# One PSUM pool with banks in fixed turns for the prologue and the first loop of a long-convolution and maxout kernel, with the first loop's tables loaded later

## The chip, the cores and the metric

The kernel runs on one core of a Trainium2 chip. A core has a matrix engine (PE, TensorE), three engines for element-wise work (DVE or VectorE, ACT or ScalarE, POOL or GpSimd), a queue engine that issues transfers (SP or SyncE), a working memory (SBUF) and a small memory that matrix products are written to (PSUM). PSUM is used here as eight banks of 128 partitions x 512 fp32. Every engine works through its own list of instructions in order; semaphores hold an instruction back until those it depends on are done. The metric is the device time of one execution in microseconds (us), the median of several runs.

## The reference

All arrays are fp32. A filter is made of a small network and a decaying window, convolved with u = x * v along the sequence (length S = 12544, four batches, 128 channels), gated with x, and fed to a maxout layer:

```
h_mlp  = np.maximum(pos_emb @ w1, 0.0) @ w2            # (S, 128), pos_emb is (S, 64)
h_filt = h_mlp * np.exp(-0.01 * pos)[:, None]
u = x * v                                              # (4, S, 128)
y = irfft(rfft(u, 2*S) * rfft(h_filt, 2*S)[None], 2*S)[:, :S]
a = (x * y).reshape(4*S, 128)
out = np.maximum(np.maximum(a @ m1, a @ m2), a @ m3) @ m_out   # m1..m3: (128, 768)
```

The weights m1 to m_out come in as float64 and are turned into fp32 on DVE.

## The kernel before

The Fourier transforms are matrix products with tables, in two stages (sizes 90 and 128). The order of the work is that of the program: each engine gets its instructions in the order in which the code writes them down, and a layer above the hardware adds the semaphore waits. It keeps them by tile: a tile from a pool is a piece of SBUF or PSUM with a name; when a pool of `bufs` tiles hands out a piece again, the new writer waits for the readers of the old one, and when a pool is closed and another opened in its place, the new one's tiles wait for all that used the old piece.

*Prologue* (before.py up to L989). PE makes the filter's network (`mlp_in`, L334; two PSUM tiles `pms` of two banks each, memset at L291) while the first units of u are loaded, multiplied on DVE (`u_mul`, L374), transposed on PE (`turn2`, L900; L379) and taken through the first stage (`early`, L918). This uses the pool `fps0`, closed at L957. A second pool `fps` (L958) has four tiles of two banks. In it run 16 products of the filter (`quad`, L909, with `first_halves`, L159: PE at L165, copy on ACT at L174 into `specH`), then the units u = 4 to 31 in pairs (two `quad`, then a `turn2` for a later pair; copies into `spec`). Each pair frees SBUF for a pair of loads (`u_load`, L362) that SP issues. Between them DVE converts the weights (`some`, L886), whose raw data POOL's queue loads. Ahead of the units, SP also issues the six first tables of the first loop (L972 and L973: `wf` and `wi`, 256 KB each, `load_dir`, L895). L994 closes the pool.

*First loop* (L1096, s = 0 to 47, NK = 45). It does the second stage, the product with the filter, and the first stage back, for one batch, two frequencies per step. It has three PSUM pools (L998 to L1000): `cps0` with three banks, `sps` with one tile of two banks (tag h) and one of one bank (tag pl), and `gps` with two banks. In step s, in this order on PE:

- `s_second(s)` (L1028, "ss"): the filter's second stage into a bank of `gps`, copied by ACT (G, L1042)
- `g_second(s)` (L555, "even product" in the text): u's second stage, PE at L156, into a bank of `cps0`; ACT copies half of it (eo, L192)
- `s_filter(s-1)` (L1045): the filter's last product, PE at L1055 into the tile h, copied by ACT (ht, L1071; for the last step L1064)
- `g_third(s-3)` (L592, "third product"): the stage back, PE at L156, into a bank of `cps0`; ACT copies it (zs, L603) and SP stores it to `zd`

ACT also swaps halves (xs, L570 and L571, for s-1). DVE does the multiplication with the filter for s-2 (L576, L580, L581), the unfolding (ab, L588) and then the butterfly of s (`g_butterfly`, L562; L186 and L187, which read the even product's bank). POOL negates a table (L1025) and stores ht. In steps 36, 37, 41 and 42 a unit of the next batch is also transposed (`u_turn`, L379) into the bank pl, and in some steps multiplied (L374).

*End of the loop* (L1133 to L1145). The last third products (of 42, 43 and 44) alternate with two late units (`unit`, L1091: two calls of `u_products`, L417, each 16 products at L427, a copy on ACT at L439, two sums on DVE at L443) and with `fold` (L1015), which multiplies m1 with m_out: transposes into a bank (L1017), a copy (w1t, L1019), a product into pl, and a last copy into `lin` (L1144). The banks for units and turns come from `banks_of` (L1001), a fixed list of six.

*Second loop and last part* (from L1148, some 310 us to the end) are not touched. Its tiles are loaded from `zd` once the last third product is stored.

Of the kernel before, what the change touches and what calls it, by code (L numbers as in the profile page):

```python
# [10 lines left out]
FP32 = mybir.dt.float32  # L11
# [4 lines left out]
PSUM = bass.MemoryType.PSUM  # L16
P = 128
# [14 lines left out]
def e(t):  # L32
    return np.exp(2j * np.pi * (t - np.floor(t)))


def stacked(c):

    top = np.concatenate([c.real, c.imag], -1)
    bottom = np.concatenate([-c.imag, c.real], -1)
    return np.concatenate([top, bottom], -2)  # L40


def tables(NB):
    S = P * N1
    k1 = np.arange(N1).reshape(2, N1 // 2).T.ravel()
    n = np.arange(NB)
    a = e(np.outer(n, k1 + 0.25) / N1)
    f1 = np.concatenate([a.real, a.imag], 1)
    up = e(np.outer(n + 0.5, k1 + 0.25) / N1)
    f1q = np.stack([np.concatenate([up.real, up.imag], 1), f1], 1)  # L50
    f1h = np.zeros((64 + HH, 2, 2 * N1))
    f1h[:HH, 0], f1h[64:, 0] = f1[:HH], f1[HH:NH]
    f1h[:HH, 1], f1h[64:, 1] = f1[HH:NH], f1[:HH]
    f4 = np.stack([a.T.real, a.T.imag], 1) / S
    f4p = f4[::2].transpose(1, 0, 2).reshape(N1, NB // 2, 2).transpose(0, 2, 1)
    f4 = np.stack([up.T.real, up.T.imag], 1) / S
    f4s = f4[::2].transpose(1, 0, 2).reshape(N1, NB // 2, 2).transpose(0, 2, 1)
    f4q = np.stack([f4p, f4s * np.array([1, -1])[:, None]], 1)
    j, t = np.arange(64), np.arange(64)
    tw = (k1[:, None, None] + 0.25) / S  # L60
    half = []
    for r in range(2):
        s2 = (127 - 2 * t - r)[None, :, None]
        half.append(stacked(e(tw * s2 + j[None, None, :] * s2 / 128)))
    fwd = np.stack(half, 2)
    half = []
    for q in range(2):
        s2 = (2 * t + q)[None, None, :]
        half.append(stacked(e(-tw * s2 - j[None, :, None] * s2 / 128)))
    inv = np.stack(half, 2)  # L70
    both = np.stack([fwd, inv], 2)
    both = both.reshape(N1 // 2, 2, P, 2, 256).transpose(0, 2, 3, 1, 4)
    both = both.reshape(N1 // 2, P, 2, 512)
    j, t = np.arange(32), np.arange(32)
    quarter = [[], []]
    for v in range(2):
        for w in range(2):
            s2 = (63 - 2 * t - v)[None, :, None]
            quarter[0].append(stacked(e(tw * s2 + (2 * j + w)[None, None, :] * s2 / 128)))
            s2 = (2 * t + w)[None, None, :]  # L80
            quarter[1].append(stacked(e(-tw * s2 - (2 * j + v)[None, :, None] * s2 / 128)))
    quarter = np.stack([np.stack(q, 1) for q in quarter], 1)
    quarter = quarter.reshape(N1 // 2, 2, 2, 2, 2, 64, 64).transpose(0, 3, 5, 2, 1, 4, 6)
    quarter = quarter.reshape(N1 // 2, P, 2, 256)
    steps = np.zeros((N1 // 2 + LATE, P, 2, 256))
    steps[:N1 // 2, :, 0], steps[LATE:, :, 1] = quarter[:, :, 0], quarter[:, :, 1]
    f32 = np.float32
    return tuple(np.ascontiguousarray(t, f32) for t in (f1q, f1h, f4q, both, steps))


@with_exitstack
def kernel(
# [21 lines left out]
    NK = N1 // 2  # L114
# [139 lines left out]
    pro = ExitStack()  # L254
# [5 lines left out]
    fin = ExitStack()  # L260
    inp0 = fin.enter_context(tc.tile_pool(name="inp0", bufs=3))
    sml = fin.enter_context(tc.tile_pool(name="sml", bufs=1))
    mps = ExitStack()
    fps = mps.enter_context(tc.tile_pool(name="fps0", bufs=2, space=PSUM))

# [18 lines left out]
    warm = sml.tile([P, 256], FP32, name="warm")  # L286
    nc.vector.memset(warm[:], 0.0)
    nc.vector.memset(win, 0.0)
    pms = [fps.tile([P, 1024], FP32, name=f"pm{i}", bufs=1) for i in range(2)]
    for pm in pms:  # L290
        nc.vector.memset(pm[32:64], 0.0)  # L291
    for h in range(2):
# [37 lines left out]
    def w2_order():  # L330
        nc.scalar.copy(w2x[:].rearrange("f (c g) -> f c g", c=GC),
                       w2_in[:].rearrange("f (g c) -> f c g", c=GC))
# [24 lines left out]
    def pools(b, u):  # L357
        if b == 0:
            return inp0 if u % 2 else inp
        return inp if u < EARLY or u % 4 < 3 else inq  # L360

    def u_load(b, u):  # L362
        c, g0 = divmod(u, NG // 4)
        ts = []
        for src in (xr, vr):
            t = pools(b, u).tile([P, 4, NB], FP32, tag=f"u{len(ts)}", name="ut")
            nc.sync.dma_start(
                t[:], src[4 * g0:4 * g0 + 4, :, c, b, :].rearrange("g p n -> p g n"))
            ts.append(t)
        us[u] = ts  # L370

    def u_mul(u):
        a, v = us[u]
        nc.vector.tensor_tensor(out=a[:], in0=a[:], in1=v[:], op=ALU.mult)  # L374
# [511 lines left out]
    def some(n):  # L886
        for _ in range(n):
            if not todo and jobs:
                todo.extend(convert(raws.pop(0), *jobs.pop(0)))
                if len(jobs) > 1:  # L890
                    raws.append(load_raw(*jobs[1], nc.gpsimd))
            if todo:
                todo.pop(0)()

    def load_dir(g, a):  # L895
        w = lwp.tile([P, 2, 2, P], FP32, tag=f"w{a}", name="wt")
        nc.sync.dma_start(w[:].rearrange("p k r m -> p (k r m)"), wt_d[g, :, a, :])
        return w
# [55 lines left out]
    for u in (0, 2):  # L954
        uts.pop(u)
    w2_order()
    mps.close()  # L957
    fps = fin.enter_context(tc.tile_pool(name="fps", bufs=4, space=PSUM))  # L958
    for f in range(0, FO, 4):
        quad([hs[:, f + i] for i in range(4)], (f1h[:, 0], f1h[:, 1]), specH[:, :, :, f:f + 4])  # L960
        u, k = divmod(f // 4, 4)
# [7 lines left out]
        some(2 if u < 2 and k < 2 else 3)  # L969
    for u in range(4):  # L970
        nc.gpsimd.tensor_copy(spec[:, 0:NS, :, 4 * u:4 * u + 4], aside[u])
    wf = {g: load_dir(g, 0) for g in range(3)}  # L972
    wi = {g: load_dir(g, 1) for g in range(3)}  # L973
    for u in range(4, NU, 2):
        t = uts.pop(u)
        for v in range(2):
            if u + 4 < NU:
                u_mul(u + 4 + v)
            at = 4 * (u + v)
            quad([t[:, 4 * v + i] for i in range(4)], (f1, f1), spec[:, :, :, at:at + 4])  # L980
            some(1)
        if u + 4 < NU:
            turn2(u + 4)
        for v in (u + 10, u + 11):
            if v < NU:
                u_load(0, v)
        some(2)
    while todo or jobs:
        some(1)  # L989
# [5 lines left out]


    cvp = pro.enter_context(tc.tile_pool(name="cvp0", bufs=3))
    cps = pro.enter_context(tc.tile_pool(name="cps0", bufs=3, space=PSUM))  # L998
    sps = pro.enter_context(tc.tile_pool(name="sps", bufs=1, space=PSUM))
    gps = pro.enter_context(tc.tile_pool(name="gps", bufs=2, space=PSUM))  # L1000
    def banks_of():  # L1001
        for pool, tag, n in ((gps, "g", 1), (gps, "g", 1), (sps, "h", 2), (gps, "g", 1),
                             (cps, "cv", 1), (gps, "g", 1)):
            yield pool.tile([P, 512 * n], FP32, tag=tag, name="ps1")[:, 0:512]

    free = banks_of()

    def bank():
# [36 lines left out]
    def s_filter(g):  # L1045


        G = Gs.pop(g)
        ps = sps.tile([P, 1024], FP32, tag="h", name="sps")
        for ri in range(2):  # L1050
            for k in range(2):
                for q in range(2):
                    for h in range(2):
                        at = 512 * q + (2 * ri + k) * D
                        nc.tensor.matmul(  # L1055
                            ps[64 * h:64 * h + 64, at:at + D],
                            G[64 * q:64 * q + 64, k, ri, :], w2x[64 * q:64 * q + 64],
                            start=(ri == 0 and k == 0), stop=True, skip_group_check=True)
        v = ps[:].rearrange("p (q m d) -> p m q d", q=2, d=D)
        if g == NK - 1:  # L1060
            hts[g] = []
            for c in range(2):
                ht = lwp.tile([P, 2, 2, D], FP32, tag="w0", name="ht")
                nc.scalar.copy(ht[:], v[:, 2 * c:2 * c + 2])  # L1064
                hts[g].append(ht)
            return
        if g % 2 and g < NK - 11:
            ht = utp.tile([P, 2, 2, 2, D], FP32, tag="uT", name="ht")
        else:
            ht = cvp.tile([P, 2, 2, 2, D], FP32, tag="ht", name="ht", bufs=2)  # L1070
        nc.scalar.copy(ht[:].rearrange("p r k q d -> p (r k) q d"), v)  # L1071
        hts[g] = ht[:, 0], ht[:, 1]
# [23 lines left out]
    for s in range(NK + 3):  # L1096
# [9 lines left out]
        if 1 <= s <= NK:  # L1106
            g_swap(s - 1)
            s_filter(s - 1)
# [22 lines left out]
        if s == NK:  # L1131
            unit(0)
            pl = sps.tile([P, 512], FP32, tag="pl", name="pl")  # L1133
# [27 lines left out]
    cps = conv.enter_context(tc.tile_pool(name="cps", bufs=1, space=PSUM))  # L1161
# [15 lines left out]
    for n, (b, i) in enumerate(tiles[:LAST]):  # L1177
# [13 lines left out]
        for f in range(NF):  # L1191
# [9 lines left out]
            h = up((b, i), f)  # L1201
# [25 lines left out]
    cps = ctx.enter_context(tc.tile_pool(name="cps2", bufs=1, space=PSUM))  # L1227
# [19 lines left out]
    for i in range(0, NT, 2):  # L1247
        h = {}
        X, Y = banks if i % 4 == 0 else banks[::-1]
        for j, (name, f) in enumerate(ORDER):  # L1250
            n = int(name[1]) - 1
# [64 lines left out]
```

## Time and profile before

| what | us |
|---|---|
| median of 3 runs | 2277.69 |
| lowest and highest run | 2275.16, 2278.18 |
| the profiled execution, its own time | 2277.68 |
| its span, first to last instruction | 2275.9 |
| PE busy in it | 2255.8 |
| prologue, first instruction to last unit's product | 0 to 114.3 |
| first loop with its end | 114.3 to about 303 |

How to read it: a page of the profile gives busy times by engine, and the chain of work that ended last. The chain by time lists start, length, and what ran ("PE ps L165 x96": 96 matmuls of line 165 into the tile ps); "issue" is time in which the engine waited for nothing that the profile shows. The timeline gives start, length, engine, line, operation and tiles, and in brackets the idle time before it and who ended that. A line of busy times by stretch gives the stretch, its length, the busy time of PE, of PE's weight loads, of DVE, ACT and POOL with their counts of instructions, then the granted clock of PE (1.00 is full), the busy share of the DMA engines and GB/s. "PEld" is PE's weight load; "SPq" a transfer's issue on SP.

### The profile page before, as it was taken

To read this page: it belongs to the slowest core of one execution; us is meant where nothing else is said; L and a number is where in the kernel's file an instruction comes from. 1 tells how busy PE (TensorE), PEld (TensorE's weight loads), DVE (VectorE), ACT (ScalarE), POOL (GpSimd) and SP (SyncE) were. 2 spreads that over 40 slices of the span, in tenths; PEclk is the share of its full clock that TensorE was granted. 3 is DMA by queue.
4 is the path that set the end of the run, shared out by engine and by line. 5 is a ranking of instruction groups with operands and counts; after the bars stand their busy time and mean duration, and the time that the engine had idled before them with its cause. 6 is when DMAs were issued, how large, how long until landed. Compare 5 with 4: busy or idle time off the path is not lost.

```text
span 2275.9 us, 68490 instructions
## 1 busy us (share of the span) xinstructions
PE 2255.8 (99%) x27855; PEld 1380.2 (61%) x27855; DVE 1560.6 (69%) x2856; ACT 1175.8 (52%) x2130; POOL 879.4 (39%) x1089
## 2 busy tenths in 40 slices
PE   9999999999999999999999999999999999999998
PEld 7889866655555556655555556655555546666665
DVE  5589967677777757667878757658878754544443
ACT  3688844466666534456666534456666522222222
POOL 1045434323333334323333333423333326666666
PEclk9999999999999999999999999999999999999999
DMA  8778999799989689889999789979999732222221
GB/s 197 174 227 279 301 198 181 138 220 239 249 219 238 172 174 185 160 194 251 236 240 233 197 167 180 168 183 247 238 236 238 199 81 56 56 71 65 58 56 22
DMA packets 473365, 411.03 MB, mean 181 GB/s; under 512 B 327993, under 2 KB 374522, under 8 KB 473050
## 3 DMA queue, kind: packets, MB, share of 16 engines
q1 hardware_dynamic: 446034, 329.50, 65.2%
q0 software_dynamic: 26224, 75.44, 11.1%
q8 instruction: 219, 3.59, 0.7%
q10 hardware_dynamic: 792, 1.72, 0.3%
q14 instruction: 96, 0.79, 0.1%
HBM read 262.84 MB, written 84.67 MB: 153 GB/s over the span
## 4 chain that ended last, share of the span: by engine, by line
PE 96%; DVE 1%; issue 0%; ACT 0%; DMA 0%; SPq 0%; POOL 0%; POOLq 0%; DVEq 0%; ACTq 0%
PE hps L156 44%; PE ops L156 19%; PE ops L827 6%; PE cps L427 5%; PE cps L156 4%; PE ps L156 4%; PE cps L494 3%; PE cps L504 3%; PE ps L165 3%; PE sps L1055 2%; PE gps L1037 2%; PE last L156 1%; PE pst L379 1%; DVE spec L443 0%; DMA xT<-in_x_dram 0%
## 5 line engine op out<-in xcount | busy, mean ns | idle before, releaser
L156 PE MATMUL hps<-gt,w_sb 128*64 128x392 f32 x6144 | 1149.6, 494 | 0.0
L764 ACT ACTIVATE hid<-hps 128x392 f32<-128x392 f32 x768 | 384.0, 500 | 698.2 <-PE hps L156 679.8
L156 PEld LDWEIGHTS hps<-gt,w_sb 128*64 128x64 f32 x6144 | 432.6, 137 | 419.4 <-issue 391.5
L767 DVE TENSOR_TENSOR hid<-hid,hps 128x392 f32<-128x392 f32 x768 | 428.4, 558 | 331.2 <-PE hps L156 319.1
L156 PE MATMUL ops<-hid,wo_sb 128*64 128x392 f32 x2304 | 480.6, 492 | 0.0
L546 POOL TENSOR_TENSOR cb<-cb,xs 128x512 f32<-128x512 f32 x135 | 174.1, 1290 | 463.5 <-DVE xs L543 339.7
L156 PEld LDWEIGHTS ops<-hid,wo_sb 128*64 128x64 f32 x2304 | 173.1, 137 | 206.1 <-issue 206.1
L519 DVE TENSOR_TENSOR cb<-cps,eo 128x512 f32<-128x512 f32 (+1 forms) x288 | 175.3, 650 | 73.4 <-ACT eo L516 73.4
L443 DVE TENSOR_TENSOR spec<-cps,high 128x360 f32<-128x360 f32 x188 | 140.1, 786 | 117.7 <-ACT high L439 117.5
L782 POOL DMA_DIRECT2D out_dram<-ot x96 | 75.3, 785 | 345.3 <-ACT ot L780 311.0
L534 ACT ACTIVATE xs<-cb 32x512 f32<-32x512 f32 x270 | 169.6, 628 | 20.6 <-DVE cb L519 11.6
L535 ACT COPY xs<-cb 32x512 f32<-32x512 f32 x270 | 166.3, 616 | 3.2
L439 ACT COPY high<-cps 128x360 f32<-128x360 f32 (+1 forms) x94 | 74.9, 796 | 176.0 <-PE cps L427 140.6
L550 DVE TENSOR_TENSOR xs<-cb 128x256 f32<-128x256 f32 x270 | 140.9, 567 | 9.5 <-POOL cb L546 9.2
L427 PEld LDWEIGHTS cps<-f1q,uT 98*64 98x64 f32 x2992 | 130.2, 137 | 27.8 <-issue 25.0
L427 PE MATMUL cps<-f1q,uT 98*64 98x90 f32 x2992 | 134.4, 241 | 1.7 <-DVE spec L443 0.5
L395 POOL COPY planes<-ut 128x784 uint16<-128x784 uint16 x90 | 76.3, 848 | 144.7 <-DVE ut L374 144.7
L527 POOL DMA_DIRECT2D zd<-cb x135 | 92.7, 687 | 62.0 <-DVE cb L519 57.3
L156 PEld LDWEIGHTS cps<-f4p,even 90*64 90x64 f32 x1552 | 90.1, 138 | 34.8 <-issue 34.0
L851 POOL DMA_DIRECT2D out_dram<-o x128 | 77.7, 612 | 51.8 <-DVE o L844 49.6
L156 PE MATMUL cps<-f4p,zt 90*64 90x49 f32 x1552 | 96.4, 222 | 0.0
L156 PE MATMUL cps<-f4p,even 90*64 90x49 f32 x1552 | 95.1, 220 | 0.0
(146 smaller groups left out, 3156.4 us busy)
## 6 DMA issues: line engine op xcount, KB each, us to landing
ht<-hd SPq DMA_DIRECT2D x264, 256.0 KB, 7.0
wt<-wq_const SPq DMA_DIRECT2D x144, 256.0 KB, 6.3
zd<-cb POOLq DMA_DIRECT2D x135, 256.0 KB, 6.3
zt<-zd SPq DMA_DIRECT2D x384, 90.0 KB, 3.0
sq<-spec SPq DMA_DIRECT2D x264, 128.0 KB, 7.0
ut<-in_xr_dram SPq DMA_DIRECT2D x128, 196.0 KB, 4.0
ut<-in_vr_dram SPq DMA_DIRECT2D x128, 196.0 KB, 4.2
xT<-in_x_dram SPq DMA_DIRECT2D x256, 98.0 KB, 3.4
```

The source lines that it names most:

```text
L156: nc.tensor.matmul(out[64 * h:64 * h + 64], lhsT[:, 64 * h:64 * h + 64], rhs, start=start, stop=stop, skip_group_check=True)
L427: nc.tensor.matmul(ps[64 * c:64 * c + 64, 256 * i + h * N1:256 * i + (h + 1) * N1], t[:, 2 * ((at + i) % 8) + h].rearrange("n r t -> n (r ...
L443: nc.vector.tensor_tensor(out=spec[:, :, a, at:at + n], in0=v[:, 1], in1=highs[0], op=op)
L519: nc.vector.tensor_tensor(out=cb[:, a, lo:hi], in0=ps[:, lo:hi], in1=eo[:, lo:hi], op=op)
L527: nc.gpsimd.dma_start(zd[b][2 * z:2 * z + 2].rearrange("k c t a f -> (k c t) a f"), zss.pop(z))
L534: nc.scalar.mul(xs[at:at + 32], xt[at + 32:at + 64], -1.0)
L535: nc.scalar.copy(xs[at + 32:at + 64], xt[at:at + 32])
L546: nc.gpsimd.tensor_tensor(out=xts[g], in0=xts[g], in1=xs[:], op=ALU.add)
L550: nc.vector.tensor_tensor(out=ab[:, q], in0=y[:, 0], in1=y[:, 1], op=(ALU.subtract, ALU.add)[q])
L764: nc.scalar.activation(h[:], pa[:, 0:N], Relu)
L767: nc.vector.tensor_tensor(out=h[:], in0=h[:], in1=pb[:, 0:N], op=ALU.max)
L827: nc.tensor.matmul(ps[64 * c:64 * c + 64, 0:H2], w, rhs[:, H2 * c:H2 * c + H2], start=start, stop=True, skip_group_check=True)
```

## The change

All eight banks are taken once, as four tiles of two banks each, `acc[0]` to `acc[3]`, from one pool that lives until the end of the first loop. `half[0]` to `half[7]` are their halves, one bank each. A small class `Banks` has the method of a pool, `tile`, but hands out given pieces in fixed turns. The tiles of the first loop are halves: even and third products take turns through half[2], half[3], half[4]; ss through half[0] and half[1]; the filter's product is acc[3], and in the last step acc[0]; pl is half[5]; `banks_of` gives half[6], half[7], half[0], half[1], one of half[2..4], half[6]. The six tables are issued on SP after the loads of units 30 and 31 (in the iterations u = 22, 24 and 26) in place of ahead of all units.

```diff
+class Banks:
+    def __init__(self, **tags):
+        self.tags = {tag: itertools.cycle(aps) for tag, aps in tags.items()}
+
+    def tile(self, shape, dtype, tag, name):
+        return next(self.tags[tag])
...
-    mps = ExitStack()
-    fps = mps.enter_context(tc.tile_pool(name="fps0", bufs=2, space=PSUM))
+    acc = pro.enter_context(tc.tile_pool(name="acc", bufs=1, space=PSUM))
+    acc = [acc.tile([P, 1024], FP32, name=f"acc{i}")[:] for i in range(4)]
+    half = [a[:, 512 * i:512 * i + 512] for a in acc for i in range(2)]
+    fps = Banks(cv=acc[:2])
...
-    pms = [fps.tile([P, 1024], FP32, name=f"pm{i}", bufs=1) for i in range(2)]
+    pms = acc[2:]
...
-    mps.close()
-    fps = fin.enter_context(tc.tile_pool(name="fps", bufs=4, space=PSUM))
+    fps = Banks(cv=acc[2:] + acc[:2])
...
-    wf = {g: load_dir(g, 0) for g in range(3)}
-    wi = {g: load_dir(g, 1) for g in range(3)}
+    wf, wi = {}, {}
...
+        if u in (22, 24, 26):
+            wf[(u - 22) // 2] = load_dir((u - 22) // 2, 0)
+            wi[(u - 22) // 2] = load_dir((u - 22) // 2, 1)
...
-    cps = pro.enter_context(tc.tile_pool(name="cps0", bufs=3, space=PSUM))
-    sps = pro.enter_context(tc.tile_pool(name="sps", bufs=1, space=PSUM))
-    gps = pro.enter_context(tc.tile_pool(name="gps", bufs=2, space=PSUM))
+    cps, gps, sps = Banks(cv=half[2:5]), Banks(g=half[0:2]), Banks(h=[acc[3]], pl=[half[5]])
+
     def banks_of():
-        for pool, tag, n in ((gps, "g", 1), (gps, "g", 1), (sps, "h", 2), (gps, "g", 1),
-                             (cps, "cv", 1), (gps, "g", 1)):
-            yield pool.tile([P, 512 * n], FP32, tag=tag, name="ps1")[:, 0:512]
+        yield from half[6:8] + half[0:2]
+        yield cps.tile([P, 512], FP32, tag="cv", name="ps1")
+        yield half[6]
...
-        ps = sps.tile([P, 1024], FP32, tag="h", name="sps")
+        ps = sps.tile([P, 1024], FP32, tag="h", name="sps") if g < NK - 1 else acc[0]
```

## The prediction

> **What bounds the kernel now.** I read the whole page first (busy times, chain), then the chain by time, then busy times by stretches, then the timeline of one step of the first loop and of its end.
>
> ```profile
> PE 2255.8 (99%) x27855; PEld 1380.2 (61%) x27855; DVE 1560.6 (69%) x2856; ACT 1175.8 (52%) x2130; POOL 879.4 (39%) x1089
> ...
> PE 96%; DVE 1%; issue 0%; ACT 0%; DMA 0%; SPq 0%; POOL 0%; POOLq 0%; DVEq 0%; ACTq 0%
> ```
>
> PE is the bound from end to end: any time in which it waits in the first 310 us moves the end by as much, and no more than PE's waits there can be won. The chain by time and the stretches show where they are:
>
> ```profile
> 50.23 9.45 PE ps L165 x239
> 59.68 2.15 issue
> ...
> 114.28 0.77 ACT spec L174
> 115.04 0.04 issue
> 115.09 0.43 PE gps L1037 x2
> 115.52 0.51 issue
> ```
>
> ```profile
> 59.60:61.90 2.30, 0.15 (x4) 0.07 (x3) 0.00 (x0) 0.27 (x1) 0.00 (x0) 1.00 1.10 322
> 61.90:65.80 3.90, 3.90 (x60) 3.90 (x61) 3.77 (x11) 1.24 (x2) 0.67 (x2) 0.56 0.28 66
> 65.80:69.00 3.20, 3.20 (x67) 2.91 (x63) 0.42 (x1) 1.81 (x3) 1.75 (x4) 1.00 0.18 24
> ```
>
> PE stops at 59.68 for 2.15 us in the middle of a product, waiting for no semaphore, with the DMA engines full (1.10), and then runs 3.9 us at a granted clock of 0.56. At 114.28 it waits for the last copy of the pool that is closed. A third stop (0.92 us, before 39.16) is at the first pool's close.
>
> The first loop has no such stop. One step, g = 193.02 being the start of its even product:
>
> ```profile
> 193.02 1.04 PE L156 MATMUL ps<-spec,wt 128*64 128x128 f32 x16
> ...
> 194.16 0.37 ACT L192 COPY eo<-ps 128x256 f32<-128x256 f32 x1 [0.35 <-PE ps L156]
> ...
> 195.84 1.01 ACT L1071 COPY ht<-sps 128x1024 f32<-128x1024 f32 x1
> ...
> 196.16 0.42 DVE L186 TENSOR_TENSOR xt<-eo,ps 128x256 f32<-128x256 f32 x1
> ...
> 196.75 0.59 ACT L603 COPY zs<-ps 128x512 f32<-128x512 f32 x1
> 196.82 1.04 PE L156 MATMUL ps<-spec,wt 128*64 128x128 f32 x16
> 196.89 0.69 DVE L576 TENSOR_TENSOR xt<-xt,ht 128x512 f32<-128x512 f32 x1
> ```
>
> PE's step is 3.81 us. ACT ends its step (zs) only at 197.34 = g+4.32, after the next product began; DVE starts at 193.08, ends its butterfly at 196.91 = g+3.89, and starts the next chain at 196.89. All three engines are full, and run staggered because every product has a bank that nobody else holds.
>
> [...] ACT reads one bank at 196.75 while PE writes another. So a wait between the two halves of a two-bank tile is not asked for by the chip. [...] here 2.15 us of idleness were followed by 0.56. [...] the page's instruction queue q8 has 219 packets in 3.59 MB (16.4 KB each), and the DMA view has none of them in 52 to 58 us and one in 58 to 60[...].
>
> **The change, part by part.**
>
> 1. *First pool's close.* The last copy no longer gates the first filter product: it goes to acc[2], free and with its inputs ready when DVE has done the last MLP tile (36.97), and PE is there at 38.24. The 0.92 us go: -0.9. PE is late in nothing else there (inputs of the next transposes are multiplied by 38.5).
>
> 2. *Tables moved.* Six loads of 256 KB (1.57 MB) leave 51.9 to 55.2[...]. At about 250 GB/s that is 6.3 us of DMA[...]. The stop (2.15) goes, and with it the slow clock: 113 matmuls took 6.23 us from 61.83, at the 0.0411 of 2.63/64 they are 4.64, so 1.6. Together -3.7. The SP queue now issues them behind the last input loads, at about 99; DMA is idle from 104 to 118 (share 0.00 to 0.03), and the first is needed at 114, so they land in time. Price if their cover fails: [...]0 to +3.7. I take 0.
>
> 3. *Start of the loop.* The first filter product needs only acc[0], copied long before, so it starts at 114.25 instead of 115.09, and the 0.51 of queued waits are hidden behind it. The built order of the second even product shows a new wait for the first one's butterfly; it starts at about 117.6 instead of 118.76: -1.1.
>
> 4. *Banks as halves of four tiles.* Here is what the diff doesn't tell. In the built program, waits are made by tile, and half[2], half[3] are one tile (acc[1]), half[4] and half[5] another. Even product s and third product s-3 take turns through half[2..4], with a period of three steps. The built waits of steps 5, 6, 7 (with their producers):
>
> ```
> step 5  even  -> acc1  waits ACT zs of third(1)      new
> step 6  even  -> acc1  waits DVE butterfly of 5      new
> step 6  DVE butterfly  waits ACT zs of third(3)      new
> step 7  even  -> acc2  no wait
> ```
>
> None of these is in the kernel before. Worked out with the offsets of the step above:
> - Steps 5, 8, ... : zs ends at g+4.32, ACT to PE takes 0.05 (267.03+1.01 to 268.09), so the next product starts at g+4.37, not 3.81: +0.56. There are 14 (5 to 44); at 38 a transpose covers it: 13 x 0.56 = 7.3.
> - Steps 6, 9, ... : the butterfly starts at g+4.37 instead of 3.14. DVE, which has no slack (its chain from L576 to butterfly is 3.08, and 0.73 more to the next L576), carries this lag through step 7 to step 8: L576 at g+5.10, then +3.81 to the next L576, then 3.08 + 0.75 to the end of that butterfly. With the steps 3.81 and 4.37 in between this is 4.56 after product 8, +0.14 from DVE to PE (305.72 to 305.86), 4.70 instead of 3.81: +0.89. There are 13 (6 to 42); 39 and 42 are covered by transposes: 11 x 0.89 = 9.8.
> - Transposes (L379) go to half[5], one tile with half[4]. Steps 36 and 42: the next even product waits for the transpose's copy (ends at g+4.81): g+4.86 instead of 4.53, +0.33 each. In step 37 the transpose waits for the butterfly (g+4.02, +0.14) instead of starting at g+2.93: +1.23; in step 41 for zs (g+4.37): +1.44. Sum 3.3. A multiplication (L374, 0.56) ahead of one such butterfly: +0.5.
> Sum of the loop: +20.9.
>
> 5. *End of the loop.* The last filter product saves its 0.79 of waiting, but DVE and ACT set that stretch, so 0 is won. The first late unit's two halves are now half[6] and half[7], one tile, and the second half waits until DVE has added up the first:
>
> ```profile
> 289.63 1.41 PE L427 MATMUL ps<-f1q,uT 98*64 98x90 f32 x32
> ...
> 291.27 1.09 PE L156 MATMUL ps<-ab,wt 128*64 128x128 f32 x16 [0.23 <-DVE xt L576]
> ...
> 293.73 1.09 DVE L443 TENSOR_TENSOR spec<-ps,high 128x180 f32<-128x180 f32 x4
> 293.76 1.09 PE L156 MATMUL ps<-ab,wt 128*64 128x128 f32 x16
> ```
>
> Behind that PE wait are queued the last two third products, at 291.27 and 293.76. The first half's adds end at about 294.3, +0.7 for DVE's lag; so the first of them goes from 291.27 to about 295.8, the second (behind a fold that waits for zs) from 293.76 to about 298.3: +4.5. Their stores, the reload and the second loop follow. The other unit has the same wait (+1.2) and the folds wait for each other's copies (+0.8). PE idles some 5.5 us, more than the 2.15 that cost it its clock: +0.7 as a middle of 0 to 1.7. Together +7.
>
> After 310 us nothing differs; what is late stays late.
>
> **Sum.** -0.9 -3.7 -1.1 +20.9 +7 = +22.2. The profiled execution took 2277.68 us (span 2275.9), the median of the three runs is 2277.69: 2299.9, I say 2300. Unknown costs: the lag on DVE 0 to 9.8, the clock 0 to 1.7, the end 4 to 8[...].
>
> **Rivals.**
> - *The half-tile waits are there but covered*: PE works ahead of its waits, as in steps whose copies end early. Then only the gains are left, -5.7: 2272, faster. It decides if zs ends 0.57 us earlier in its step (g+3.76), and the unit's adds before 290.3. Against it: ACT has 0.35 of idle time in a step of 3.81 and serves in order, and the adds stand behind eleven DVE operations. 4%.
> - *Only the first kind of wait bites*, DVE catching up in the longer steps: +7.3, transposes 3, end 6, gains -5.7: +10.6, 2288. For it: DVE gets 0.56 of slack per period. Against it: the lag is 1.2. 17%.
> - *The stop moves with the tables*[...]: +3.7, 2304. For it: the same burst; against it: no weight loads on POOL's queue beside it. 15%.
> - *Waits add up further* (ACT late behind a late DVE): another 7 to 12, about 2310. 8%.
> - *Gains and losses cancel*: 4%. The forecast itself: 52%.
>
> **Numbers.** 0.2% (4.6 us) is about what a measurement of this kernel tells from none. Faster 0.04, same 0.04, slower 0.92. The range goes from the second rival to between the third and fourth: 2287 to 2309.
>
> **What would show it.** Right: in the first loop, PE waiting 0.5 us for ACT zs and 0.9 for DVE xt, each once in three steps, so that three steps take 12.9 instead of 11.4 us; a PE wait of several us at L437 for DVE spec at the loop's end; no stop of PE at 60, clock 1.00 there. Wrong: steps of 3.81 throughout, or a stop with half clock near 100.

## The result, and the profile after

The changed kernel takes 2304.96 us (median of 4 runs, 2302.07 to 2310.09) against 2276.43 us for the kernel before (4 runs): a ratio of 1.0128, 95% interval 1.0107 to 1.0149, so 1.3% slower. Its profiled execution took 2304.03 us, with a span of 2302.2 us; that of before had 2275.9 us. So 26.3 us are to be found between the two traces. The page after:

```profile
PE 2267.7 (98%) x27855; PEld 1380.4 (60%) x27855; DVE 1559.2 (68%) x2856; ACT 1176.3 (51%) x2130; POOL 869.9 (38%) x1089
...
PE 92%; DVE 4%; ACT 2%; issue 1%; DMA 0%; SPq 0%; POOL 0%; DVEq 0%; POOLq 0%; ACTq 0%
```

The number of matmuls is the same, PE is busy for 11.9 us more (2255.8 before), and PE's share of the last chain has fallen from 96% to 92%, while DVE's rose from 1% to 4% and ACT's from 0 to 2%: somewhere PE waits for them, and somewhere its matmuls got longer.

The chain by time after shows the prologue and the first steps (all lines of after.py are 8 to 10 higher than in before.py: L173 was L165, L1047 was L1037):

```profile
49.31 13.79 PE acc L173 x352
63.10 1.01 PE acc L389 x8
...
104.16 5.11 PE acc L173 x128
109.28 1.00 PE acc L1047 x16
110.28 0.95 PE acc L164 x16
111.23 0.90 PE acc L1047 x16
112.12 0.02 issue
112.15 0.38 ACT G L1052
112.53 0.05 issue
112.58 1.11 PE acc L164 x16
```

The row of 13.79 us is the one that was cut in two by the stop at 59.68; it starts 0.92 us earlier than before (50.23), and has no gap. The first filter product of the loop follows the last unit's product with no wait. The second even product (112.58) is 6.2 us earlier than before (118.76), though it waits here. The chain names ACT's G, which ended 0.05 us before; the wait that the prediction took from the built program is for the first product's butterfly on DVE, which ended at 112.43. The stretches of before's stop, after:

```profile
59.60:61.90 2.30, 2.30 (x66) 2.30 (x62) 2.27 (x6) 1.34 (x2) 1.28 (x3) 1.00 0.02 3
61.90:65.80 3.90, 3.90 (x85) 3.61 (x83) 1.93 (x5) 2.78 (x4) 1.88 (x3) 1.00 0.26 59
65.80:69.00 3.20, 3.20 (x68) 2.91 (x64) 0.42 (x1) 2.10 (x3) 0.00 (x0) 1.00 1.05 290
```

PE is busy throughout, at full clock; the DMA engines, full in the first of these stretches before (1.10), are nearly idle there (0.02).

The first loop, timeline of three steps (even products at 189.57, 193.86 and 197.72, the next at 202.09):

```profile
188.93 0.59 ACT L613 COPY zs<-acc 128x512 f32<-128x512 f32 x1
...
189.57 1.09 PE L164 MATMUL acc<-spec,wt 128*64 128x128 f32 x16 [0.40 <-ACT zs L613]
...
193.30 0.41 DVE L195 TENSOR_TENSOR xt<-eo,acc 128x256 f32<-128x256 f32 x1
...
193.86 1.09 PE L164 MATMUL acc<-spec,wt 128*64 128x128 f32 x16 [0.27 <-DVE xt L195]
...
197.72 1.04 PE L164 MATMUL acc<-spec,wt 128*64 128x128 f32 x16
...
198.25 0.42 DVE L194 TENSOR_TENSOR xt<-eo,acc 128x256 f32<-128x256 f32 x1 [1.67 <-ACT zs L613]
```

Each kind of wait that the built program promised is there: PE for zs of a third product in the other half, PE for the butterfly of the step before, and DVE's butterfly for zs. The steps, as differences of the starts of even products from the timelines:

| step | before | after | predicted |
|---|---|---|---|
| 8, 11, 14, ... | 3.81 | 4.38 | 4.37 |
| 9, 12, 15, ... | 3.80 | 4.29 | 4.70 |
| 10, 13, 16, ... | 3.81 | 3.86 | 3.81 |

And the end of the loop. Busy times by stretch, from the last even product (295.36) to the first matmuls of the second loop (330.86), in the columns explained under "How to read it":

```profile
295.36:304.10 8.74, 5.83 (x128) 4.97 (x128) 7.93 (x15) 6.53 (x12) 2.90 (x6) 1.00 0.70 189
304.10:314.30 10.20, 7.59 (x70) 6.37 (x70) 2.34 (x7) 2.33 (x6) 0.00 (x0) 0.50 0.24 73
314.30:317.70 3.40, 1.96 (x25) 1.42 (x25) 1.20 (x4) 0.79 (x3) 0.00 (x0) 1.00 0.42 112
317.70:328.00 10.30, 8.63 (x77) 6.36 (x77) 1.64 (x3) 2.92 (x7) 2.77 (x3) 0.50 0.41 107
328.00:330.86 2.86, 2.82 (x81) 2.65 (x77) 1.84 (x4) 1.14 (x2) 0.00 (x0) 1.00 0.00 0
```

The same part of the kernel before, all of it at full clock:

```profile
283.79:306.50 22.71, 19.71 (x379) 16.21 (x376) 15.24 (x33) 14.17 (x31) 3.15 (x6) 1.00 0.64 173
```

The timeline of the late unit after, its two halves being the two lines of L437:

```profile
300.40 0.79 PE L437 MATMUL acc<-f1q,uT 98*64 98x90 f32 x16
...
305.36 0.59 DVE L453 TENSOR_TENSOR spec<-acc,high 128x180 f32<-128x180 f32 x2
306.09 1.47 PE L437 MATMUL acc<-f1q,uT 98*64 98x90 f32 x16 [4.90 <-DVE spec L453]
307.32 1.95 PE L164 MATMUL acc<-ab,wt 128*64 128x128 f32 x16
```

The second half of the late unit waits 4.90 us for DVE's sums of the first half, as forecast. But the column of the clock says more: PE then runs at 0.50 for 10.2 us, and a second time for 10.3 us. The same 16 matmuls of L437 take 0.79 us at 300.40 and 1.47 at 306.09.

The sum of the two traces: to the second even product -6.2; from there to the last even product +17.8 (182.8 against 165.0); end of the loop +12.8 (35.5 against 22.7); the rest of the execution +2.0 (1971.3 against 1969.4). Together +26.4.

### The profile page after: what moved, and what is told of

Its sections match the earlier page's. It is cut to its first block, busy times and chain, and to the rows that moved or that the text cites. A ratio compares the mean times of both kernels' runs of the same rounds, so it can differ in the third digit from the quotient of the medians.

```text
span 2302.2 us, 68505 instructions
## 1 busy us (share of the span) xinstructions
PE 2267.7 (98%) x27855; PEld 1380.4 (60%) x27855; DVE 1559.2 (68%) x2856; ACT 1176.3 (51%) x2130; POOL 869.9 (38%) x1089
## 4 chain that ended last, share of the span: by engine, by line
PE 92%; DVE 4%; ACT 2%; issue 1%; DMA 0%; SPq 0%; POOL 0%; DVEq 0%; POOLq 0%; ACTq 0%
PE hps L164 44%; PE ops L164 19%; PE ops L837 6%; PE cps L437 5%; PE cps L164 4%; PE cps L504 3%; PE acc L164 3%; PE acc L173 3%; PE cps L514 3%; PE last L164 1%; PE acc L1065 1%; ACT ht L1081 1%; PE acc L389 1%; DVE ab L598 1%; DVE xt L591 1%
## 5 line engine op out<-in xcount | busy, mean ns | idle before, releaser
L164 PE MATMUL hps<-gt,w_sb 128*64 128x392 f32 x6144 | 1149.2, 494 | 1.1 <-DVE hid L777 1.0
L164 PEld LDWEIGHTS hps<-gt,w_sb 128*64 128x64 f32 x6144 | 430.5, 137 | 422.6 <-issue 392.0
L164 PE MATMUL ops<-hid,wo_sb 128*64 128x392 f32 x2304 | 480.1, 492 | 0.0
L164 PEld LDWEIGHTS ops<-hid,wo_sb 128*64 128x64 f32 x2304 | 172.0, 137 | 207.2 <-issue 207.2
L437 PEld LDWEIGHTS cps<-f1q,uT 98*64 98x64 f32 x2992 | 131.5, 138 | 28.4 <-issue 25.6
L437 PE MATMUL cps<-f1q,uT 98*64 98x90 f32 x2992 | 135.9, 243 | 1.9 <-DVE uT L420 1.5
L164 PEld LDWEIGHTS cps<-f4p,even 90*64 90x64 f32 x1552 | 89.7, 138 | 34.9 <-issue 33.8
L164 PE MATMUL cps<-f4p,zt 90*64 90x49 f32 x1552 | 96.3, 222 | 0.0
L164 PE MATMUL cps<-f4p,even 90*64 90x49 f32 x1552 | 95.0, 220 | 0.0
```

Of the source, the lines that this page charges most:

```text
L164: nc.tensor.matmul(out[64 * h:64 * h + 64], lhsT[:, 64 * h:64 * h + 64], rhs, start=start, stop=stop, skip_group_check=True)
L437: nc.tensor.matmul(ps[64 * c:64 * c + 64, 256 * i + h * N1:256 * i + (h + 1) * N1], t[:, 2 * ((at + i) % 8) + h].rearrange("n r t -> n (r ...
```

## The experiments

The theory: waits are kept by tile, so halves of one tile that take turns wait for each other's readers, and the stop at the end costs PE's clock too. The rivals: the later tables collide with something; the fixed turns cost, not the tiles' borders; the end is set by DVE and ACT whatever PE's clock is; the stop at 60 us belongs to single executions and not to the tables.

All ratios are to the kernel before, run beside each experiment on the same chip. Its medians there were 2276.73 us (for tables_late, mid_apart, before_cv_tile and end_busy), 2277.12 (ends_apart, end_busy2, all_apart, before_again) and 2276.65 (before_cv_one, apart_tables_early).

**tables_late**

```diff
 (kernel before)
-    wf = {g: load_dir(g, 0) for g in range(3)}
-    wi = {g: load_dir(g, 1) for g in range(3)}
+    wf, wi = {}, {}
...
+        if u in (22, 24, 26):
+            wf[(u - 22) // 2] = load_dir((u - 22) // 2, 0)
+            wi[(u - 22) // 2] = load_dir((u - 22) // 2, 1)
```

> The kernel before with the six table loads moved behind the last units, and nothing else. Theory (banks that share a tile cost the time; the move of the tables is a gain): PE's stop of 2.15 us at 60 and the half clock after it go, 2276.4 - 3.7 = 2272.7, no new stop near 100 us. Rival 1 (the tables, loaded later, collide with other transfers or come late for the first loop): 2276 or more, with a stop of PE between 90 and 120 us.

Measured: 2275.00 us, ratio 0.9989 (0.9980 to 0.9997). The stop at 60 is gone, and none is near 100: the rival of colliding tables falls. But the medians differ by 1.7 us and not by 3.7. In the trace the second loop starts 3.7 us earlier than in before's (302.81 against 306.50), and the rest of that execution is 1.3 us longer. Which of the two is the rule was left to before_again.

**mid_apart**

```diff
 (changed kernel; acc[1] and acc[2] come from a pool "part" of their own)
+    part.close()
+    one = pro.enter_context(tc.tile_pool(name="one", bufs=1, space=PSUM))
+    for i in (2, 3, 4, 5):
+        half[i] = one.tile([P, 512], FP32, name=f"one{i}")[:]
     cps, gps, sps = Banks(cv=half[2:5]), Banks(g=half[0:2]), Banks(h=[acc[3]], pl=[half[5]])
```

> The changed kernel, but the four banks of acc[1] and acc[2] are opened again as four tiles of one bank each when the first loop begins; turns, order of work and bank contents as in the changed kernel. Theory: the waits between even products, butterflies and third products go, steps are 3.8 us throughout, the loop gives back its 17.7 us: 2305 - 17.7 = 2287, while the stop of about 4.9 us of the late unit stays. Rival 2 (it is the fixed turns, in place of a pool's choice, that cost): 2305, steps as in the changed kernel.

Measured: 2279.71 us, ratio 1.0013 (1.0007 to 1.0020). PE's two costliest waits from the loop on; the second stands after the second loop's start:

```profile
PE acc L440 <- DVE spec L456: 6.2, 2, 4.9
PE hps L164 <- DVE hid L780: 1.9, 1, 1.9
```

Not one wait for zs or the butterfly is left, and all ordinary steps are 3.80 or 3.81. The turns are the same as in the changed kernel, so the rival of fixed turns falls: what costs is the tile's border. The gain was 25 us by medians, not 17.7. Its loop takes 164.8 us (-18.0), and most of the other part came from the end of the loop: 30.4 us instead of 35.5. Less of that end runs at half clock (6.8 and 3.4 us), and of the folds' waits 0.2 us is left. So the terms do not simply add up. (The span of this trace is 21.5 us shorter than after's: its second loop has the wait of 1.9 us above, and the two matmuls of L164 after it took 0.80 us, where eight take 1.50 otherwise.)

**before_cv_tile**

```diff
 (kernel before)
-    cps = pro.enter_context(tc.tile_pool(name="cps0", bufs=3, space=PSUM))
+    cps = pro.enter_context(tc.tile_pool(name="cps0", bufs=1, space=PSUM))
+    two = cps.tile([P, 1024], FP32, name="two")[:]
+    cps = Banks(cv=[two[:, 0:512], two[:, 512:1024], cps.tile([P, 512], FP32, name="one")[:]])
```

> The kernel before, with two of the three banks for even and third products made one tile of two banks; all else as before. Theory: the same waits as in the changed kernel appear in every third step, +17 us in the loop and up to 1 at the folds: 2276.4 + 17.5 = 2294. Rival 2 (turns, pools or the tables): three banks in turn are still three banks, 2276.

Measured: 2293.19 us, ratio 1.0071 (1.0056 to 1.0086). Two of three banks in one tile make the kernel before 16.5 us slower; that they also come in fixed turns costs nothing, as mid_apart shows. Its steps are those of the changed kernel (4.38, 4.29, 3.86). One thing was not expected: its tables are loaded early, and its trace has no stop at 60:

```profile
50.85 13.79 PE ps L173 x352
64.64 1.01 PE pst L387 x8
```

**before_cv_one**

```diff
 (kernel before)
+    all3 = cps.tile([P, 1536], FP32, name="all3")[:]
+    cps = Banks(cv=[all3[:, 512 * i:512 * i + 512] for i in range(3)])
```

> The kernel before, with all three banks for even and third products in one tile of three banks; all else as before. Theory (each use of a tile waits for the last reader of the tile, whichever bank it read): every butterfly waits for zs of the same step (g + 4.37) and every even product for that butterfly (0.75 long, 0.14 to PE): steps of 5.25 instead of 3.81 from step 4 on, 41 x 1.44 less some 3 us at transposes = +56, 2277 + 56 = 2333. Rival (each shared tile costs a delay of about 0.57 once per use, as in every third step of the changed kernel): steps of 4.38, +23, 2300.

Measured: 2339.79 us, ratio 1.0279 (1.0264 to 1.0295). A step of its timeline:

```profile
203.04 0.59 ACT L611 COPY zs<-all 128x512 f32<-128x512 f32 x1
...
203.66 0.42 DVE L194 TENSOR_TENSOR xt<-eo,all 128x256 f32<-128x256 f32 x1 [1.81 <-ACT zs L611]
204.00 0.41 DVE L195 TENSOR_TENSOR xt<-eo,all 128x256 f32<-128x256 f32 x1
...
204.56 1.09 PE L164 MATMUL all<-spec,wt 128*64 128x128 f32 x16 [1.26 <-DVE xt L195]
```

The three engines that ran staggered now run in turn: copy, butterfly, product. The step is 5.28 us, where the rule of tiles gave 5.25 and the rival 4.38. From the second to the last even product the loop takes 224.4 us (+59.4, forecast +56), and its end 24.2 (+1.5, not forecast). Of the surplus in the loop, 1.9 us is step 3, which has the wait too (4.78 instead of 2.93 us), and 1.2 is the step, 0.03 longer than forecast 41 times.

Its trace has a stop near 60 again: PE stops after the same 239 matmuls as before, at 60.42, for 1.38 us, and the 113 matmuls after it run at full clock (4.58 us; from 40 to 110 us PE is busy for 68.62 of 70.00 us, at 1.00).

**ends_apart**

```diff
 (changed kernel; acc[0] is opened again as two tiles of one bank)
-        yield from half[6:8] + half[0:2]
+        for i in (0, 1, 6, 0):
+            yield half[i]
         yield cps.tile([P, 512], FP32, tag="cv", name="ps1")
-        yield half[6]
+        yield half[1]
...
-        ps = sps.tile([P, 1024], FP32, tag="h", name="sps") if g < NK - 1 else acc[0]
+        ps = sps.tile([P, 1024], FP32, tag="h", name="sps")
```

> The changed kernel, but acc[0] is opened again as two tiles of one bank, and the late units and the last filter product use the banks that they had in the kernel before; acc[1] and acc[2] stay shared. Theory: the stop of 4.9 us of the late unit and the clock that it costs go, the loop's waits stay: 2305 - 12.7 + 1 for the folds that still share tiles = 2293. Rival (DVE and ACT, late from the loop, set the end whatever the units' banks are): 2298 or more.

Measured: 2295.01 us, ratio 1.0080 (1.0066 to 1.0094). The stop of 4.9 us is gone, the loop's waits are as in the changed kernel. The end takes 27.3 us, 8.2 less than after and 4.6 more than before: folds and turns still wait for each other in the shared tiles, and once more 10.3 us run at half clock, though no single wait just before them is longer than 0.7 us:

```profile
295.47:310.60 15.13, 12.77 (x228) 10.13 (x228) 11.37 (x26) 10.38 (x22) 2.90 (x6) 1.00 0.64 180
310.60:320.90 10.30, 9.31 (x98) 7.74 (x98) 2.87 (x4) 2.76 (x7) 1.83 (x2) 0.50 0.46 112
320.90:322.80 1.90, 1.86 (x57) 1.69 (x53) 0.62 (x2) 0.62 (x2) 0.94 (x2) 1.00 0.00 0
```

**end_busy and end_busy2**

```diff
 (changed kernel)
+    def keep_busy(at, n):
+        for _ in range(n):
+            halves_mm(half[at][:, 0:P], eye[:], eye[:], True, True)
...
     def unit(u):
         for h in range(2):
+            if h:
+                keep_busy(*((5, 22), (7, 6))[u])
             u_first(u, 2 * h, 2)
```

In end_busy the counts are 36 and 10.

> The changed kernel with 72 unneeded matmuls (4.7 us at full clock) ahead of the second half of the first late unit and 20 (1.3 us) ahead of that of the other; they write free banks. Theory: of the 12.7 us that the end of the loop costs, about 7 are PE at half clock for two spells of 10.24 us after its stops; kept busy, PE keeps its clock there, and 5 to 7 us go: 2299. Rival 3 (the waits alone set the end, PE's clock is hidden behind ACT and DVE): 2305 or a little more.

> As end_busy, with 22 and 6 calls in place of 36 and 10, since each call took 0.223 us and the 36 held the unit up for 3 us. 4.9 and 1.3 us of unneeded matmuls now fill the waits and no more. Theory: the half clock after the waits costs 6 to 7 us, and they go: 2298.5. Rival (the clock is hidden behind ACT and DVE): 2303 or more.

Measured: end_busy 2303.60 us, ratio 1.0120 (1.0103 to 1.0137). Its 36 calls took 8.03 us (144 matmuls, 0.056 us each), so they held the unit up for 3 us: the count was mis-sized, and the time says little about the clock. end_busy2: 2299.43 us, ratio 1.0099 (1.0085 to 1.0113). Its timeline:

```profile
302.52 0.79 PE L437 MATMUL acc<-f1q,uT 98*64 98x90 f32 x16
303.14 4.97 PE L164 MATMUL acc<-eye 128*64 128x128 f32 x88
308.20 0.84 PE L437 MATMUL acc<-f1q,uT 98*64 98x90 f32 x16
308.84 1.08 PE L164 MATMUL acc<-ab,wt 128*64 128x128 f32 x16
```

The wait is as long as in the changed kernel, now filled with unneeded work, and the matmuls after it take 0.84 and 1.08 us instead of 1.47 and 1.95. The whole end runs at full clock:

```profile
297.48:326.53 29.05, 26.23 (x486) 22.27 (x487) 14.97 (x32) 13.93 (x29) 4.64 (x8) 1.00 0.50 134
```

It takes 29.05 us, 6.45 less than after. So of +12.8 us, 6.4 are half clock and 6.3 waits. The rival that DVE and ACT hide the clock falls.

**all_apart**

```diff
 (changed kernel; only acc[3] stays, units and last filter product as in ends_apart)
+    part.close()
+    one = pro.enter_context(tc.tile_pool(name="one", bufs=1, space=PSUM))
+    for i in (0, 1, 2, 3, 4, 5):
+        half[i] = one.tile([P, 512], FP32, name=f"one{i}")[:]
```

> The changed kernel, but only acc[3] stays a tile of two banks; the other six banks are opened again as six tiles of one bank when the first loop begins, and the late units and the last filter product use the banks that they had in the kernel before. Theory: neither the loop's nor the end's waits are left, the gains of the tables and of the first pool's close stay: mid_apart's 2279.7 less the 7.7 us by which its end of the loop is longer than before's = 2272 (2270.5 to 2274), below both kernels. Rival (opening the banks again costs as much as the pools did, and other waits come in their place): 2275 or more.

Measured: 2273.08 us (21 runs), ratio 0.9983 (0.9977 to 0.9990): a little faster than both kernels. Its ordinary steps are 3.80 or 3.81, its end takes 23.2 us, and the clock is full in all of it. From 110 to 280 us PE is busy for 169.85 of 170.00 us and ACT for 150.23: ACT copies from banks while PE writes others, each of the six a tile of its own. Opening the banks again costs little: the second stage of the loop follows the last unit's product with 0.15 us of issue between.

**before_again and apart_tables_early**

before_again is the kernel before, unchanged, for a second trace. apart_tables_early is all_apart with the table loads ahead of the units, as before has them.

> The kernel before once more, for its trace. Theory of the tables as put in the prediction: the stop of 2.15 us at 60 with 3.4 us of half clock belongs to the kernel and is there again. Rival: [...]is gone or elsewhere; then it is no part of the difference of the medians, or only of some executions.

> all_apart with the six table loads back where the kernel before has them (ahead of the units). Theory of the prediction's second step[...]: a stop of 1.4 to 2.2 us near 60 us comes back, with or without half clock: 2273.1 + 1.4 to 3.7 = 2275.5. Rival ([...]as in before_cv_tile, which kept the tables and had no stop): 2273, no stop.

Measured: before_again 2276.87 us (one run); apart_tables_early 2274.40 us, ratio 0.9991 (0.9983 to 0.9999). The chain by time of before_again:

```profile
51.03 9.44 PE ps L165 x239
60.48 1.41 issue
61.88 4.58 PE ps L165 x113
```

The same view of apart_tables_early:

```profile
49.22 9.52 PE acc L173 x241
58.74 1.28 issue
60.02 4.56 PE acc L173 x110
```

In before_again the stop is at the same matmul (after 239), but it lasts 1.41 us instead of 2.15, and the 113 matmuls after it run at full clock (4.58 us, where the first trace had 6.23). With the tables early in the kernel of all_apart a stop comes back, 1.28 us, again at full clock. (That trace also has 3.4 us at half clock from 301.1, around the start of the second loop, where 16 matmuls of L440 took 1.47 us against 0.79 at 297.68, so its span does not measure the stop.)

So a stop is in four of the five traces with early tables and in none of the seven with late ones. That the fifth, before_cv_tile, has none is hardly due to its program: before_cv_one, which has the stop, is the same up to the first loop. The stop then belongs to single executions with early tables, 1.28 to 2.15 us long where it comes. What PE waits for in it is not shown.

The early tables cost 1.7 us by tables_late's medians, with an interval clear of 1. The ratios of apart_tables_early and all_apart differ by as much (0.0008, 1.8 us), but their intervals overlap.

## Why the prediction was right, point by point

The forecast was 2300, the time 2304.96, in the range and on the right side. By its own steps, on the traces:

| step | forecast | trace |
|---|---|---|
| 1 first pool's close | -0.9 | -0.9 |
| 2 tables moved | -3.7 | -4.1 |
| 3 start of the loop | -1.1 | -1.2 |
| 4 loop | +20.9 | +17.8 |
| 5 end of the loop | +7 | +12.8 |
| after 310 us | 0 | +2.0 |

Steps 1 and 3 hold (50.23 to 49.31 for the first; -4.1 is 114.25 to 109.28 less the first step; the third is the rest of -6.2 at the second even product). The total is off by less than the end alone: the loop was forecast 3.1 us too dear and the end 5.8 us too cheap, and that they offset each other is luck.

*Step 2* holds against the trace it was made for, but that trace was a costly one: the stop is 1.41 us and no half clock in a second trace of the same kernel, and moving the tables alone gained 1.7 us on medians. I priced one execution's stop as the kernel's. That the six loads set it off through the instruction queue was my estimate from that trace alone (no packet of q8 from 52 to 58 us, one at 59.0, PE again at 61.83); no run shows it. Rival "the stop moves with the tables" is wrong: none of the seven traces with late tables has it.

*Step 4*, the main term: the mechanism is shown from both sides (mid_apart takes it away, before_cv_tile and before_cv_one put it in). The first kind of wait cost 0.58 a step (forecast 0.56); steps 36 to 43, with the transposes, 4.7 (forecast 3.3 for the transposes and 0.89 and 0.56 for the waits of steps 36 and 41, together 4.75). The second kind was mis-sized: 0.48 instead of 0.89, over steps 6 to 33 5.3 us. The failed sentence is that DVE "has no slack". Its chain starts (L586) were at 189.98 and 193.63, then after the late butterfly 198.92 and 202.50: 3.65 and 3.58 apart when nothing holds it, where I had 3.81, the step that PE imposed. The trace of before could have told: in two of its steps (193.08 to 200.69) DVE is busy for 7.13 of 7.61 us, so 0.24 us of each step is free. Two steps of catching up at about 0.2 each are the missing 0.4. The rival in which DVE catches up entirely was wrong too: 0.48 is left.

*Step 5*: the waits were right in place and size (forecast 4.5 + 1.2 + 0.8 = 6.5; end_busy2, which leaves them and keeps the clock, has 6.3). The failed term is the clock, +0.7 forecast, 6.4 measured. I took the one spell that before's trace showed (3.4 us at half clock, 0 to 1.7 us of cost) as the measure; here half clock, once granted, stayed for 10.2 us and again for 10.3, with PE busy for 7.59 and 8.63 us of it. The spells in the first 330 us of the traces differ in length: 3.4 us in before, after a stop of 2.15 us, 6.8 and 3.4 us in mid_apart, 10.2 and 10.3 us in the changed kernel. In the end of the changed kernel PE also has a short wait for ACT at several of the small products (four, of 0.3 to 0.7 us). In ends_apart such waits alone, without the stop of 4.9 us, came before 10.3 us at half clock; what keeps the clock down was not tried.

*After 310 us*: the +2.0 is within what executions differ by. From the start of the second loop's first products to the end, before has 1969.4, before_again 1970.7, all_apart 1970.5, after 1971.3, apart_tables_early 1971.8; only mid_apart, with its wait of 1.9 us there, has more (1973.5).

## What to carry to other kernels

Before halves of a tile are used as buffers in turn, list for each use who reads the other half last: the wait is for that reader, and the built program shows it before any run. A tile should be as large as the thing that is written and freed together, not as large as the memory that is saved. And price a stop of PE with the half clock that may follow it: here 6.3 us of waits came with 6.4 us lost at half clock.

## What was not expected of the hardware

- Half clock does not follow from the length of a stop alone. Stops of PE of 1.28 (apart_tables_early), 1.38 (before_cv_one) and 1.41 us (before_again) were followed by full clock, one of 2.15 us (before) by 3.4 us at half, and stops of 4.9 us came with 6.8 us (mid_apart) and 10.2 us (after). In ends_apart waits of 0.7 us and less came before 10.3 us at half clock. Yet before_cv_one, in which PE waits 1.26 us in nearly every step and idles for 40 of 170 us, ran its loop at full clock:

```profile
110.00:280.00 170.00, 130.09 (x2594) 112.30 (x2594) 105.47 (x217) 107.94 (x191) 50.48 (x95) 1.00 0.64 189
```

- A wait costs more than its length: in the changed loop PE is idle for 12.2 us of 182.8 and its busy time is 170.6 instead of 164.7 us for the same matmuls at full clock. That is 5.9 us over 27 waits, 0.2 us for each. The profile models the ends of matmuls, so part of this may be how it counts idle time; the step itself is 0.58 us longer where 0.40 is listed as idle.
- The stop of PE near 60 us is in one execution and not in another: before_cv_one and before_cv_tile run the same program up to the first loop, with the tables loaded in the same place, and only the first has the stop (1.38 us).
